# ScalarE seeds the next unit's accumulator before it squares and stores the last unit, in the first MLP layer of a gated FNet kernel

## The chip, the cores and the metric

The kernel runs on one core of a Trainium2 chip. The metric is the device time of one execution in microseconds (us), as the median of several runs. The engines are written as the profile has them: PE is TensorE's matmuls, PEld its weight loads, DVE is VectorE, ACT is ScalarE, and SP is the engine that issues most of the transfers.

## The reference

With S = 2048 tokens, D = 512 and F = 1792, all in float32, where `xn` is the layer-normalised input:

```python
xn = layernorm(x)
a, b = xn @ hid_re.T, xn @ hid_im.T
s = seq_re @ a - seq_im @ b
h = relu(xn @ w1 + b1) ** 2
out = x + s * silu(h @ w2 + b2)
```

The change lies in the line that computes `h`.

## The kernel before, in words

Every product of matrices is cut into blocks of 2 by 2 and computed with seven block products instead of eight, with sums of blocks on both sides. Each operand is held as a high and a low part, and each block product takes three passes (high by high, high by low, low by high). The stages follow one another on TensorE: layer norm and the first transform, the second transform, eight units of the hidden transform (`YUnit`), 28 units of the first MLP layer (`HUnit`), the second MLP layer with the gate, and a tail. The order of the instructions on each engine is the order in which the program is written, since the scheduler is set to manual. What an engine does beside the units is set by hand in tables (`H_SIDE` for this stage): names of steps that load an operand, form its sums and split it into high and low part. Of each operand ScalarE makes the high part (line 136) and VectorE then the low part (line 139).

**A unit of the first layer** covers two of the 14 blocks of 128 hidden features for one of the four chunks of 512 tokens: 4 chunks by 7 pairs make 28 units. Unit n has four accumulators of 256 columns in PSUM, A, B, C and D, and units of even and odd n use different banks. Its seven products, each of six matmuls of 256 columns on line 790, go to A (1, then 2), to D (7), to B (6, then 5, then 3) and to C (4). The sums between products are made by seeding: ScalarE copies minus A into B before product 6 is added on top (line 146, the step `seed("B", "A")`), and minus B into C before product 4. Below, these two are called seed B and seed C.

What is read out of a unit, all into a buffer `h` of four blocks:

- `m7`: ScalarE copies D (line 146).
- `c11`: ScalarE applies bias and relu to A after product 2 (line 848).
- `c22`: VectorE adds B after product 5 to what m7 left (line 860 or 800). Product 3 goes into the same accumulator, so it waits for c22.
- `c21`: VectorE subtracts C after product 4 (line 860 or 803).
- `c12`: ScalarE applies bias and relu to B after product 3 (line 848).
- For the eleven units in `ACT_PAIR` (4, 5, 6, 8, 10, 12, 14, 16, 18, 21, 25) ScalarE also does the relu of the two lower blocks (a second line 848, 512 columns) and squares all 1024 columns. For the others VectorE squares the lower two blocks (line 875), and ScalarE squares 512 columns.
- `square()`: that square on ScalarE (line 879), and behind it on ScalarE's queue the transfer of `h` to HBM (line 880), from where the second layer loads it (line 760).

**The loop over the units** interleaves two units. Pass n, here called round n, issues for unit n the products 1, 7, 6 and 2, and for unit n-1, named `before` in the code, the rest. TensorE's order in a round is product 1 of unit n, then 5 and 4 of n-1, then 7 and 6 of n, then 3 of n-1, then 2 of n. ScalarE's order in a round is seed B of n, c11 of n-1, the splits of the table's second column, m7 and seed C of n, c12 of n-1 (with the relu of the lower blocks), and last the square and the store of n-1. VectorE's order is c22 and c21 of n-1 and then the table's second column: low parts, and the sums for later ones. In the texts below T(n) is the time at which TensorE starts product 5 of unit n-1 in round n, right after product 1 of unit n.

Of the kernel before, what the change touches and what calls it, by code (L numbers as in the profile page):

```python
# [130 lines left out]
def fnet_gated_kernel(ctx, tc, x, xt, ct, wd, w1, w2, b1, b2, out):  # L131
# [274 lines left out]
    def go(*names):  # L406


        for v in names:
            if v[0] == "h" and int(v[1:]) >= NTC * NP:  # L410
                continue
            if v not in making:
                making[v] = makers[v[0]](int(v[1:]))
            next(making[v])
# [469 lines left out]
    def bias(m, n, cols=slice(0, 2)):  # L884

        m = m.rearrange("p (k e) -> p k e", k=2)[:, cols]
        b = BIASED[n] * 256
        copy(m, b2s[:, None, b:b + 256].to_broadcast([P, cols.stop - cols.start, 256]))

    def outer(m, k, n, cols=(0, 1)):  # L890

        p = n % NP
        a, b = PRODUCTS[k]
        for i in cols:
            for a_, b_ in PASSES:
                nc.tensor.matmul(m[:, i * 256:(i + 1) * 256], ready[n][:, a_, H_SLOT[a], i * P:(i + 1) * P],  # L896
                                 W2[p][:, b_, b], start=p == 0 and i == 0 and (a_, b_) == (HI, HI) and k not in BIASED,
                                 stop=p == NP - 1 and (a_, b_) == (LO, HI), skip_group_check=True)
# [59 lines left out]
    for u in range(2):  # L958
        unit = YUnit(u)
# [32 lines left out]
    before = None  # L992
    for u in range(2, NC):
        n = 2 * u + 2
        unit = YUnit(u)
# [26 lines left out]
        before = unit  # L1022


    class Banks(dict):
# [4 lines left out]
        def __missing__(self, k):  # L1030
# [2 lines left out]
            self[k] = bank(tag, f"m{k}_o{self.c}")  # L1033
            return self[k]

    for n in range(NTC * NP):
        unit = HUnit(n)
        first, second, later = H_SIDE.get(n, ((), (), ()))
        go(*first)
        unit.products(1)  # L1040
        unit.seed("B", "A")
        before.c11()
        before.products(5)
        before.c22()
        before.products(4)
        before.c21()
        go(*second)
        unit.products(7)
        unit.m7()
        unit.products(6)  # L1050
        unit.seed("C", "B")
        before.products(3)
        before.c12()
        if n == NTC * NP - 1:
            ms = Banks(0)
            for k in (2, 4):
                bias(ms[k], k)
        unit.products(2)
        before.square()
        go(*later)  # L1060
        before = unit

    outer(ms[1], 1, 0)
    before.c11()
    before.products(5)
    before.c22()
# [123 lines left out]
def _launch(arrays, out_shape):  # L1190
    import numpy as np
    import concourse.bacc as bacc
    from concourse.bass_utils import run_bass_kernel_spmd

    nc = bacc.Bacc("TRN2", target_bir_lowering=False, num_devices=1, dynamic_dma_scratch_size=1024)
    feed, args = {}, []
    for name, v in arrays.items():
        v = np.ascontiguousarray(v)
        feed[f"in_{name}"] = v
        args.append(nc.dram_tensor(f"in_{name}", v.shape, mybir.dt.from_np(v.dtype), kind="ExternalInput").ap())  # L1200
    args.append(nc.dram_tensor("out_0", out_shape, F32, kind="ExternalOutput").ap())
    with tile.TileContext(nc, schedule_with_timeline_sim=True) as tc:
        fnet_gated_kernel(tc, *args)
    r = run_bass_kernel_spmd(nc, [feed], core_ids=[0])
    return r.results[0]["out_0"]
# [25 lines left out]
```

## Time and profile before

| what | value |
|---|---|
| median of 3 runs | 673.04 us (672.74 to 673.34) |
| the profiled execution's own time | 672.81 us |
| its span, first to last instruction | 671.0 us |
| PE busy | 665.1 us, 99% of the span |
| DVE busy | 596.4 us, 89% |
| ACT busy | 380.2 us, 57% |
| first-layer rounds | 403 to 536 us of the span |

The profile is of one execution. A row of its timeline gives the start in us from the span's start, the duration, the engine, the line, the operation and the tiles it writes and reads; several equal instructions in a row are merged, with their count. In square brackets stands the idle time of the engine before the row and what ended it. The end of a matmul is modelled, so a group of matmuls reads a little longer than the distance to the next group's start.

### The profile page before, as it was taken

What the parts mean: (1) busy time and instruction counts of PE and PEld (TensorE: products, weight loads), DVE (VectorE), ACT (ScalarE), POOL (GpSimd) and SP (SyncE); (2) the same over time, 40 slices, a digit from 0 to 9 for tenths busy, and PEclk for the clock granted to TensorE, in tenths of its full rate; (3) what the DMA queues carried; (4) which work ended last, traced back from release to release, by engine and by line L of the source; (5) the groups of instructions that cost most, each with busy time, mean ns of one, the idle gap of its engine ahead of it and who ended that gap; (6) DMA issues with size and microseconds to landing.
All of it is one profiled execution on the core that took longest, in us unless ns stands there. A gap on an engine that the chain in (4) does not pass through costs nothing.

```text
span 671.0 us, 13184 instructions
## 1 busy us (share of the span) xinstructions
PE 665.1 (99%) x5437; PEld 646.3 (96%) x5437; DVE 596.4 (89%) x831; ACT 380.2 (57%) x524; POOL 8.8 (1%) x11
## 2 busy tenths in 40 slices
PE   9999999999999999999999999999999999999997
PEld 6888889999999999999999999999999999999997
DVE  7997888999999999899899988977877889999997
ACT  6855664634445454444464557888778865454451
POOL 0000000000000000000000000000000000101010
PEclk9999999999999999999999999999999999999999
DMA  8635497646556774759588558565755866777775
GB/s 292 226 115 206 145 347 269 220 142 224 200 167 226 252 282 162 262 186 346 184 303 278 181 189 317 202 251 205 271 182 198 324 243 214 190 218 190 219 205 156
DMA packets 51739, 150.82 MB, mean 225 GB/s; under 512 B 4960, under 2 KB 19552, under 8 KB 50272
## 3 DMA queue, kind: packets, MB, share of 16 engines
q1 hardware_dynamic: 43568, 129.28, 56.9%
q10 hardware_dynamic: 6208, 18.88, 7.1%
q0 software_dynamic: 1904, 1.84, 1.9%
q8 instruction: 42, 0.69, 0.4%
q14 instruction: 17, 0.14, 0.1%
HBM read 101.98 MB, written 47.99 MB: 223 GB/s over the span
## 4 chain that ended last, share of the span: by engine, by line
PE 96%; DVE 1%; ACT 1%; DMA 0%; issue 0%; ACTq 0%; SPq 0%; DVEq 0%
PE m L382 34%; PE m_o L896 15%; PE r_B L790 13%; PE r_A L790 9%; PE pq_b L397 8%; PE r_C L790 4%; PE r_D L790 4%; PE m_last L896 4%; PE pq_ba L397 2%; PE pq_bc L397 2%; PE pq_bb L397 2%; DVE z L1146 0%; DMA x<-in_x 0%; DVE z L946 0%; ACT h L848 0%
## 5 line engine op out<-in xcount | busy, mean ns | idle before, releaser
L382 PEld LDWEIGHTS m<-g,xc 128*128 128x128 f32 x2016 | 228.6, 188 | 0.1
L382 PE MATMUL m<-g,xc 128*128 128x256 f32 x2016 | 228.7, 276 | 0.0
L136 ACT ACTIVATE g<-u 128x1792 fp32r<-128x1792 f32 (+2 forms) x65 | 99.0, 1523 | 126.9 <-PE m L382 89.0
L139 DVE TENSOR_TENSOR g<-u,g 128x1792 fp32r<-128x1792 f32 (+2 forms) x66 | 116.9, 1772 | 19.8 <-ACT g L136 19.2
L896 PE MATMUL m_o<-w,g 128*128 128x256 f32 x882 | 100.5, 276 | 0.0
L896 PEld LDWEIGHTS m_o<-w,g 128*128 128x128 f32 x882 | 100.3, 188 | 0.0
L136 ACT ACTIVATE g<-hr 128x1792 fp32r<-128x1792 f32 (+2 forms) x31 | 48.2, 1565 | 40.0 <-PE m_o L896 16.8
L790 PE MATMUL r_B<-xT,w 128*128 128x256 f32 x504 | 66.6, 277 | 0.4 <-ACT r_B L146 0.4
L397 PE MATMUL pq_b<-g,xc 128*128 128x512 f32 x240 | 65.2, 391 | 0.4 <-DVE small L247 0.4
L790 PEld LDWEIGHTS r_B<-xT,w 128*128 128x128 f32 x504 | 61.5, 188 | 0.5 <-ACT r_B L146 0.5
L139 DVE TENSOR_TENSOR g<-hr,g 128x1792 fp32r<-128x1792 f32 (+2 forms) x31 | 56.7, 1837 | 2.9 <-ACT g L136 2.8
L397 PEld LDWEIGHTS pq_b<-g,xc 128*128 128x128 f32 x240 | 44.7, 188 | 10.7 <-ACT g L136 0.8
L790 PE MATMUL r_A<-xT,w 128*128 128x256 f32 x336 | 42.8, 276 | 0.0
L790 PEld LDWEIGHTS r_A<-xT,w 128*128 128x128 f32 x336 | 40.2, 188 | 0.0
L790 PE MATMUL r_B<-wdp,yg 128*128 128x256 f32 x288 | 35.8, 277 | 0.0
L304 DVE TENSOR_TENSOR u<-u 128x512 f32<-128x512 f32 x48 | 32.8, 684 | 1.9 <-DMA u<-in_ct 1.9
L790 PEld LDWEIGHTS r_B<-wdp,yg 128*128 128x128 f32 x288 | 34.1, 188 | 0.0
L896 PE MATMUL m_last<-w,g 128*128 128x256 f32 x294 | 33.5, 276 | 0.0
L896 PEld LDWEIGHTS m_last<-w,g 128*128 128x128 f32 x294 | 33.4, 188 | 0.0
L139 DVE TENSOR_TENSOR yg<-yraw,yg 128x1792 fp32r<-128x1792 f32 x13 | 26.2, 2018 | 0.6 <-ACT yg L136 0.6
L136 ACT ACTIVATE yg<-yraw 128x1792 fp32r<-128x1792 f32 x13 | 22.2, 1708 | 5.8 <-DVE yraw L313 5.3
L790 PE MATMUL r_D<-xT,w 128*128 128x256 f32 x168 | 23.6, 276 | 0.0
(192 smaller groups left out, 877.8 us busy)
## 6 DMA issues: line engine op xcount, KB each, us to landing
u<-in_ct SPq DMA_DIRECT2D x63, 512.0 KB, 3.8
hd<-h ACTq DMA_DIRECT2D x28, 512.0 KB, 3.9
hr<-hd SPq DMA_DIRECT2D x28, 512.0 KB, 3.8
wdp<-wdd SPq DMA_DIRECT2D x8, 896.0 KB, 6.5
yraw<-pqd SPq DMA_DIRECT2D x13, 512.0 KB, 5.9
pqd<-c SPq DMA_DIRECT2D x6, 1024.0 KB, 6.3
w<-w1d SPq DMA_DIRECT2D x6, 896.0 KB, 8.2
y<-y ACTq DMA_DIRECT2D x8, 512.0 KB, 5.2
```

Source lines behind the costliest of these rows:

```text
L136: nc.scalar.activation(hi, src, AF.Copy)
L139: nc.vector.tensor_tensor(lo, src, hi.bitcast(F32), op=ALU.subtract)
L304: nc.vector.tensor_tensor(t[:, 0:2], r[:, 0:1].to_broadcast([P, 2, 256]), r[:, 1:3], op=ALU.add)
L382: nc.tensor.matmul(ps[:, d], w[:, a_, d * P:(d + 1) * P], halves(mv(b_)), start=first and d == 0 and (a_, b_) == (HI, HI), stop=last and ( ...
L397: nc.tensor.matmul(accs[c][k], w, part[c, j][:, b_, 2 * h:2 * h + 2], start=j == 0 and h == 0 and (a_, b_) == (HI, HI), stop=j == NJ - 1 a ...
L790: nc.tensor.matmul(self.region(REGION[k]), w, mv, start=i == 0 and k in (1, 7), stop=i == len(ops) - 1, skip_group_check=True)
L896: nc.tensor.matmul(m[:, i * 256:(i + 1) * 256], ready[n][:, a_, H_SLOT[a], i * P:(i + 1) * P], W2[p][:, b_, b], start=p == 0 and i == 0 an ...
```

## The change

At the top of a round, the square and the store of a unit come behind the seed B of the unit two further on: the loop remembers one more unit, `behind`. In round n ScalarE now issues seed B of n, then the square and the store of unit n-2, then c11 of unit n-1 and the rest as before. The call at the end of the round goes away. For unit 26 the call stands behind the loop, and ScalarE's order there is the same as before. No instruction is added or removed.

```diff
+    behind = None
     for n in range(NTC * NP):
         unit = HUnit(n)
...
         unit.products(1)
         unit.seed("B", "A")
+        if behind:
+            behind.square()
         before.c11()
         before.products(5)
         before.c22()
...
         unit.products(2)
-        before.square()
         go(*later)
-        before = unit
+        before, behind = unit, before

     outer(ms[1], 1, 0)
+    behind.square()
     before.c11()
```

The first place is ScalarE in rounds 5 and 6. In the names, `r5_B` is accumulator B of unit 5, `h4` is the buffer that units 4 and 5 share, `xT2` and `xT3` are the input operands of the second chunk of tokens, and `hd` is the place of h in HBM. Before:

```order
L146 ACTIVATE r5_B_4737<-r5_A_4730 128x256
L848 ACTIVATE h4_4703<-r4_A_4666,b1s_65 128x256
L136 ACTIVATE xT2_4754<-xr2_4266 128x768
L136 ACTIVATE xT2_4754<-xs2_4691 128x1024
L146 ACTIVATE h4_4703<-r5_D_4765 128x256
L146 ACTIVATE r5_C_4779<-r5_B_4737 128x256
L848 ACTIVATE h4_4703<-r4_B_4673,b1s_65 128x256
L848 ACTIVATE h4_4703<-h4_4703,b1s_65 128x2x256
L879 ACTIVATE h4_4703<-h4_4703 128x1024
L880 DMA hd0_4_96<-h4_4703 128x1024
L146 ACTIVATE r6_B_4808<-r6_A_4801 128x256
```

And with the change:

```order
L146 ACTIVATE r5_B_4735<-r5_A_4728 128x256
L879 ACTIVATE h2_4579<-h2_4579 128x2x256
L880 DMA hd0_3_95<-h2_4579 128x1024
L848 ACTIVATE h4_4703<-r4_A_4664,b1s_65 128x256
L136 ACTIVATE xT2_4754<-xr2_4266 128x768
L136 ACTIVATE xT2_4754<-xs2_4691 128x1024
L146 ACTIVATE h4_4703<-r5_D_4765 128x256
L146 ACTIVATE r5_C_4779<-r5_B_4735 128x256
L848 ACTIVATE h4_4703<-r4_B_4671,b1s_65 128x256
L848 ACTIVATE h4_4703<-h4_4703,b1s_65 128x2x256
L146 ACTIVATE r6_B_4806<-r6_A_4799 128x256
```

The seed of `r6_B` now follows unit 4's relu directly, and the square and store of unit 3 have come in between the seed of `r5_B` and everything else of round 5: c11 of unit 4, the two splits of `xT2`, and seed C.

The second place is ScalarE in rounds 22 and 23, where `g0` and `g1` are the first operands of the second layer, split in two parts. Before:

```order
L146 ACTIVATE r23_B_5878<-r23_A_5871 128x256
L848 ACTIVATE h22_5845<-r22_A_5806,b1s_65 128x256
L136 ACTIVATE g1_5896<-hr1_1_5618 128x1024
L136 ACTIVATE g1_5896<-hr1_0_5617 128x768
L146 ACTIVATE h22_5845<-r23_D_5901 128x256
L146 ACTIVATE r23_C_5915<-r23_B_5878 128x256
```

And with the change:

```order
L146 ACTIVATE r23_B_5876<-r23_A_5869 128x256
L879 ACTIVATE h20_5717<-h20_5717 128x1024
L880 DMA hd3_0_113<-h20_5717 128x1024
L848 ACTIVATE h22_5845<-r22_A_5804,b1s_65 128x256
L136 ACTIVATE g1_5896<-hr1_1_5616 128x1024
L136 ACTIVATE g1_5896<-hr1_0_5615 128x768
L146 ACTIVATE h22_5845<-r23_D_5901 128x256
L146 ACTIVATE r23_C_5915<-r23_B_5876 128x256
```

Here a square of 1024 columns (unit 21 is in `ACT_PAIR`) and its store stand between seed B and seed C of the same unit.

## Rows read from the trace of the kernel before

**Rows 1.** The page, part 1: busy time, share of the span, instructions.

```profile
PE 665.1 (99%) x5437; PEld 646.3 (96%) x5437; DVE 596.4 (89%) x831; ACT 380.2 (57%) x524; POOL 8.8 (1%) x11
```

**Rows 2.** Waits of PE in the span: total us, times, longest us.

```profile
PE r_B L790 <- ACT r_B L146: 0.4, 1, 0.4
```

**Rows 3.** Timeline of PE and PEld, rounds 6 and 7.

```profile
426.70 0.84 PE L790 MATMUL r_B<-xT,w 128*128 128x256 f32 x6
...
428.74 1.52 PE L790 MATMUL r_B<-xT,w 128*128 128x256 f32 x12
...
431.46 0.84 PE L790 MATMUL r_B<-xT,w 128*128 128x256 f32 x6
...
434.02 1.66 PE L790 MATMUL r_B<-xT,w 128*128 128x256 f32 x12 [0.35 <-ACT r_B L146]
435.52 1.52 PE L790 MATMUL r_A<-xT,w 128*128 128x256 f32 x12
...
428.63 1.43 PEld L790 LDWEIGHTS r_B<-xT,w 128*128 128x128 f32 x12
...
434.02 1.46 PEld L790 LDWEIGHTS r_B<-xT,w 128*128 128x128 f32 x12 [0.55 <-ACT r_B L146]
```

**Rows 4.** Timeline of ACT, from the end of round 4 to round 7.

```profile
421.29 0.63 ACT L879 ACTIVATE h<-h 128x512 f32<-128x512 f32 x1
...
422.33 0.37 ACT L146 ACTIVATE r_B<-r_A 128x256 f32<-128x256 f32 x1 [0.40 <-PE r_A L790]
422.61 0.47 ACT L848 ACTIVATE h<-r_A,b1s 128x256 f32<-128x256 f32 x1
422.96 0.85 ACT L136 ACTIVATE xT<-xr 128x768 fp32r<-128x768 f32 x1
...
424.91 0.39 ACT L146 ACTIVATE r_C<-r_B 128x256 f32<-128x256 f32 x1
425.54 0.47 ACT L848 ACTIVATE h<-r_B,b1s 128x256 f32<-128x256 f32 x1 [0.24 <-PE r_B L790]
425.92 0.72 ACT L848 ACTIVATE h<-h,b1s 128x512 f32<-128x512 f32 x1
426.66 1.06 ACT L879 ACTIVATE h<-h 128x1024 f32<-128x1024 f32 x1
427.76 0.33 ACTq L880 DMA_DIRECT2D hd<-h  x1
428.13 0.37 ACT L146 ACTIVATE r_B<-r_A 128x256 f32<-128x256 f32 x1 [0.40 <-ACT h L879]
...
433.60 0.37 ACT L146 ACTIVATE r_B<-r_A 128x256 f32<-128x256 f32 x1 [0.40 <-ACT h L879]
```

**Rows 5.** Timeline of DVE in rounds 5 and 6, five instructions left out.

```profile
423.85 0.96 DVE L139 TENSOR_TENSOR xT<-xr,xT 128x768 fp32r<-128x768 f32 x1
...
428.71 0.42 DVE L800 TENSOR_TENSOR h<-r_B,h 128x256 f32<-128x256 f32 x1
```

**Rows 6.** Timeline of ACT and DVE in rounds 2 and 3.

```profile
409.17 1.71 ACT L136 ACTIVATE w<-w1raw 128x1792 fp32r<-128x1792 f32 x1 [0.36 <-DVE w1raw L313]
...
410.91 2.02 DVE L139 TENSOR_TENSOR w<-w1raw,w 128x1792 fp32r<-128x1792 f32 x1
...
414.37 0.48 DVE L860 SCALAR_TENSOR_TENSOR h<-r_B,b1s,h 128x256 f32<-128x256 f32 x1
```

**Rows 7.** Timeline of ACT and DVE in rounds 8 and 9.

```profile
438.94 1.70 ACT L136 ACTIVATE w<-w2raw 128x1792 fp32r<-128x1792 f32 x1
...
440.67 2.03 DVE L139 TENSOR_TENSOR w<-w2raw,w 128x1792 fp32r<-128x1792 f32 x1 [1.02 <-ACT w L136]
...
443.75 0.42 DVE L800 TENSOR_TENSOR h<-r_B,h 128x256 f32<-128x256 f32 x1
```

**Rows 8.** Timeline of SP and DVE: a stored h loaded again, and used.

```profile
513.98 0.37 SPq L760 DMA_DIRECT2D hr<-hd  x1
...
532.35 0.68 DVE L310 TENSOR_TENSOR hr<-hr 128x512 f32<-128x512 f32 x1
```

## The prediction

> **What bounds the kernel now.** I read the page's busy times first. TensorE is busy 99% of the span [rows 1], so only a stall of TensorE, or the end of one, can move the time. The list of waits comes second: in the 28 rounds of this stage TensorE waits once, on a ScalarE write to accumulator B [rows 2]. The timeline of TensorE, third, shows the place and the price. A round is 42 matmuls in 4.76 us (T(6) = 426.70, T(7) = 431.46 [rows 3]), 0.68 us per product and 1.36 per group of twelve. Product 6 starts 2.04 after T (426.70, 428.74), so in round 7 it was due at 431.46 + 2.04 = 433.50. It started at 434.02, and the group after it at 435.52 instead of 434.86. **The stall cost 0.66 us.** The timeline of ScalarE, fourth, says why: seed B of unit 7 ran from 433.60 to 433.97, behind the relu, square and store of a unit in `ACT_PAIR` [rows 4].
>
> From this stall I take the rule for all others. The weight load stood still too, and for 0.55 us [rows 3]; it normally leads its matmul by 0.11 (428.63, 428.74). It began 0.05 after the seed's end. So a late operand costs: its end, plus 0.05, minus the due time of the weight load, plus 0.03 for the restart. Here that is 434.02 - 433.39 + 0.03 = 0.66.
>
> **What the change removes.** Seed B no longer stands behind a square (1.10 us up to the store's issue, [rows 4]: 426.66, 427.76) and the issue (0.37: 427.76, 428.13). It then follows product 1 at once. The end of product 1 reads T + 0.16 (a group of twelve reads 1.52 and the next starts after 1.36), and ScalarE starts 0.04 after a TensorE end (c12 at 425.54, its product from 428.74 - 4.76 = 423.98, reading 1.52). So seed B starts at T + 0.20 where ScalarE is free, far ahead of T + 2.04. **The stall of 0.66 goes.** That is all there is to gain; where seeds were late by less (428.13 in round 6) TensorE did not wait.
>
> **What it adds.** ScalarE used the time before product 1 ended to square and issue. Now it waits there, and square and issue come after seed B, ahead of c11, the splits and seed C. Its steps, start to start, from [rows 4]: seed 0.28 (422.33, 422.61); square of 512 columns 0.66 (0.63 and the 0.04 before an issue); square of 1024 columns 1.10; issue 0.37; c11 0.35 (422.61, 422.96); a split in two parts with m7 behind it 1.95 (422.96, 424.91). Two kinds of deadline come after that, and I went through all rounds for both.
>
> *Kind one: c22, through VectorE.* VectorE's low part waits for ScalarE's high part, c22 of the next round stands behind it in VectorE's queue, and product 3 waits for c22. Product 3's weight load is due 0.68 - 0.11 after the start of its group, in round 6 at 428.74 + 0.57 = 429.31.
>
> - Unit 5. In round 5, T = 421.94. Seed 422.14, square 422.42, issue 423.08, c11 423.45, split of `xT2` 423.80 instead of 422.96. Its end is 424.65, VectorE starts at 424.69 instead of 423.85 [rows 5]. From there to c22 of unit 5 VectorE runs seven instructions without a gap, so c22 moves from 428.71 to 429.55 and ends at 429.97. Stall: 430.02 - 429.31 + 0.03 = **0.74**.
> - Unit 2. In round 2, T = 407.66 (two rounds before 417.18, itself two before T(6)). c11 at 409.17, split at 409.52 instead of 409.17; its low part at 409.52 + 1.71 + 0.04 = 411.27 instead of 410.91, and c22 of unit 2 at 414.73 instead of 414.37 [rows 6]. It ends at 415.21; due 429.31 - 3 x 4.76 = 415.03. Stall: **0.26**.
> - Units 8 and 14, alike. T(8) = 435.52 + 1.36 = 436.88. A square of 1024: split at T + 0.20 + 0.28 + 1.10 + 0.37 + 0.35 = 439.18 instead of 438.94; VectorE waited for this split already (1.02 us idle), so c22 moves by 0.24 to 443.99 and ends at 444.41 [rows 7]. Due: 436.88 + 4.76 + 2.04 + 0.57 = 444.25. Stall 0.24 each, **0.48**.
>
> *Kind two: seed C.* It reads B, and product 5 of the next round adds to B, so product 5's weight load, due at T + 4.65, waits for it. With a square of 1024 and a split in two parts, seed C starts at T + 0.20 + 0.28 + 1.10 + 0.37 + 0.35 + 1.95 = T + 4.25 and releases at T + 4.25 + 0.39 + 0.05 = T + 4.69.
>
> - Rounds 10, 12, 16 and 18: late by 0.04, which costs 0.07 with the restart. That is within what 0.01 us rows can tell, so I take 0.03 each, **0.12**, between 0 and 0.28.
> - Rounds 23 and 27. The round before also has a split in two parts (with a square of 512, seed C at T + 3.81), then c12 (0.28 later, as a seed), the second relu (0.38 later: 425.54, 425.92) and 0.62 for it (0.72 less an overlap of 0.10), so seed B starts at T + 0.33 and everything 0.13 later: 0.17 + 0.03 = 0.20 each, **0.40**.
>
> The stores go out 0.5 to 1.1 us later in 26 rounds, on ScalarE's queue. The loads of h that follow have cover: unit 2's is issued at 513.98 and used at 532.35 [rows 8]. Were that gone, a load would delay VectorE's sums and then TensorE, 1 us at most. SP's queue keeps its order, so I cost this at nothing. Seed B also waits for the c12 before it on its own engine now, which ends before product 1 in all rounds but the ones above; nothing.
>
> **The sum.** 0.74 + 0.26 + 0.48 + 0.12 + 0.40 = 2.00 us of new stalls, less 0.66, is **+1.3 us**. After this stage TensorE runs without a wait to the tail, so the shift stays. Against the profiled execution's 672.81 that makes 674.15; the median of the runs is 0.23 above that execution, so **674.4 us**.
>
> One price is open: how soon the square may start behind the seed. No row has that pair. If it starts as c11 does behind a seed, it is 0.28, which I take, since both read what nobody is writing. If it had to wait for the seed's end and a hand-over (0.37 + 0.04), each of the ten late places would be 0.13 later, +1.3 us more. If ScalarE did not stand still for the issue (0.37), only unit 5 would be late, by 0.37.
>
> **A measurement of this kernel can tell about 0.2%, 1.35 us, from no change.** My sum lies on that bound.
>
> **The rivals.**
> 1. *The weight load goes ahead of the wait.* The matmul alone would wait, and each stall would be 0.14 smaller: 0.60 + 0.12 + 0.20 + 0.12 + 0 = 1.04, net +0.4, 673.4 us. Against it: in the one stall on record the weight load stood still for 0.55 us [rows 3]. That row is of a wait on ScalarE; none is of a wait on VectorE in these rounds. [...] Chance 0.12.
> 2. *Not slower: the issue does not hold ScalarE.* If the next activation passes the waiting store, c11 and the splits come 0.37 earlier; only unit 5 stalls, by 0.37, and the net is -0.3, 672.7 us. It decides at 0.37 us in unit 5's chain. Against it: in [rows 4] the activation behind an issue always starts after it (427.76, 428.13), with the square before it as the releaser. With no new stall at all it is 672.4, still no 0.2%. Chance 0.08.
> 3. *The square waits for the seed.* Ten places 0.13 later each: 675.7 us. For it: nothing shown; against it, c11 overlaps a seed in every round. Chance 0.13.
> 4. *Something outside the stage gains*, over 1.35 us: I see no cause. Chance 0.02. That the change does nothing is excluded by the order of the instructions.
>
> **How the numbers follow.** The forecast has 0.65. Ten places read to about 0.05 each, partly together, give it 673.8 to 675.0, about half above 674.39, the bound. Slower: 0.34 of the forecast and rival 3, 0.47. Within 0.2%: 0.31, 0.12 and 0.08, 0.51. Faster: 0.02. The range leaves out rival 2, most of rival 4 and the upper part of rival 3: 673.3 to 675.4.
>
> **What would show it.** In the profile of the changed kernel the wait at product 6 of unit 7 is gone, and seed B starts about 0.2 us after T in most rounds. TensorE's waits are on VectorE at product 3 of units 5 (the longest, about 0.7), 2, 8 and 14, and on ScalarE's seed C at product 5 after rounds 23 and 27. VectorE's idle time behind ScalarE's splits grows. I am wrong in kind if TensorE has no wait on VectorE there, or if a wait shows up in the second layer; wrong in size only if the places are these and the sum is not about 2 us.

## The result and the profile after

The changed kernel takes **675.98 us** (median of 6 runs, 675.46 to 676.71), the kernel before 673.22 in the same comparison: a ratio of 1.0042 (95% interval 1.0029 to 1.0055). It is slower, by 2.8 us where +1.3 was forecast, and lies 0.6 us above the top of the range (675.4).

The page's first part, of the changed kernel, for PE:

```profile
PE 668.3 (99%) x5437; PEld 647.7 (96%) x5437; DVE 596.4 (88%) x831; ACT 379.3 (56%) x524; POOL 8.8 (1%) x11
```

Against [rows 1] the other engines did the same work in nearly the same time (ScalarE 0.9 us less); TensorE's 5437 matmuls read 3.2 us more. The span is 674.3 us (671.0 before). The waits of PE and PEld between 400 and 545 us, in the changed kernel (total us, times, longest):

```profile
PE r_B L790 <- DVE h L800: 0.5, 1, 0.5
...
PEld r_B L790 <- DVE h L800: 0.9, 2, 0.7
PEld r_B L790 <- ACT r_C L146: 0.4, 2, 0.2
PEld r_B L790 <- DVE h L860: 0.2, 1, 0.2
```

The wait on seed B [rows 2] is gone. In its place stand waits on VectorE's c22 (lines 800 and 860) and on seed C, as forecast. How much of the time lies in the stage is read from two groups of TensorE's timeline, the first product 5 (round 1) and product 3 of unit 27, the last product of the stage. Of the kernel before:

```profile
402.90 0.84 PE L790 MATMUL r_B<-xT,w 128*128 128x256 f32 x6
...
534.91 0.87 PE L790 MATMUL r_B<-xT,w 128*128 128x256 f32 x6
```

and of the changed kernel, with rounds 6 and 12 between:

```profile
403.52 0.84 PE L790 MATMUL r_B<-xT,w 128*128 128x256 f32 x6
...
429.69 0.84 PE L790 MATMUL r_B<-xT,w 128*128 128x256 f32 x6
431.04 0.96 PE L790 MATMUL r_B<-xT,w 128*128 128x256 f32 x6 [0.52 <-DVE h L800]
...
462.33 0.97 PE L790 MATMUL r_B<-xT,w 128*128 128x256 f32 x6
463.14 0.87 PE L790 MATMUL r_C<-xT,w 128*128 128x256 f32 x6
463.85 0.87 PE L790 MATMUL r_D<-xT,w 128*128 128x256 f32 x6
...
538.20 0.87 PE L790 MATMUL r_B<-xT,w 128*128 128x256 f32 x6
```

The distance of the two groups, **the stage's length** from here on, is 132.01 us before and 134.68 after: +2.67, nearly all of the 2.8. (The spans of the two traces differ by 3.3. The other 0.6 lies ahead of the stage, where both kernels run the same instructions: the first product 5 starts at 402.90 and 403.52, and between 402.80 and 403.52 in all traces of this case. So kernels are compared by the stage's length.) Two things are to be seen in the middle rows. Product 3 of unit 5 (431.04), due at 429.69 + 0.68 = 430.37, is late by 0.67, and its second matmul by another 0.11, 0.78 in all: the largest new stall, forecast at 0.74. And in round 12 the groups behind a small wait (462.33) stay 0.71 us apart (463.14, 463.85), where a group of six otherwise takes 0.68. The single matmuls' starts in the trace say it more finely: 113.4 ns from one to the next (the mean of the stage that has no wait, below), but 117.7 ns behind this wait, for 40 matmuls. That was in no row the prediction used. Below, such a run of matmuls is called a slow stretch.

Summed over the stage from these single starts: the waits come to 2.34 us after and 0.63 before (+1.71), and the time of the slow matmuls above 113.4 ns each to 1.09 us after and 0.15 before (+0.94). Together +2.65.

A slow stretch doesn't need a wait. Of the 0.15 us before, 0.11 lies at the end of the stage, where the first matmuls of the second layer (line 896) come in between. In the kernel before, no wait stands ahead of these groups, and they are 0.70 to 0.71 apart:

```profile
531.40 0.87 PE L896 MATMUL m_o<-w,g 128*128 128x256 f32 x6
532.11 0.87 PE L790 MATMUL r_B<-xT,w 128*128 128x256 f32 x6
532.81 0.87 PE L790 MATMUL r_C<-xT,w 128*128 128x256 f32 x6
```

In all thirteen traces of this case a stretch begins at this same matmul: the group of six on the line of the second layer reads 0.87 us in each, where one at the usual pace reads 0.84.

### The profile page after: what moved, and what is told of

Its sections match the earlier page's. It is cut to its first block, busy times and chain, and to the rows that moved or that the text cites. A ratio compares the mean times of both kernels' runs of the same rounds, so it can differ in the third digit from the quotient of the medians.

```text
span 674.3 us, 13210 instructions
## 1 busy us (share of the span) xinstructions
PE 668.3 (99%) x5437; PEld 647.7 (96%) x5437; DVE 596.4 (88%) x831; ACT 379.3 (56%) x524; POOL 8.8 (1%) x11
## 4 chain that ended last, share of the span: by engine, by line
PE 96%; DVE 1%; DMA 1%; ACT 1%; issue 0%; SPq 0%; DVEq 0%
PE m L382 34%; PE m_o L896 15%; PE r_B L790 14%; PE r_A L790 9%; PE pq_b L397 8%; PE r_C L790 4%; PE r_D L790 4%; PE m_last L896 4%; PE pq_ba L397 2%; PE pq_bc L397 1%; PE pq_bb L397 1%; DMA x<-in_x 1%; DVE z L1149 0%; DVE z L946 0%; DVE z L951 0%
## 5 line engine op out<-in xcount | busy, mean ns | idle before, releaser
L790 PE MATMUL r_B<-xT,w 128*128 128x256 f32 x504 | 68.4, 279 | 0.6 <-DVE h L800 0.5
L790 PE MATMUL r_C<-xT,w 128*128 128x256 f32 x168 | 23.8, 277 | 0.0
```

Source lines behind the costliest of these rows:

```text
L790: nc.tensor.matmul(self.region(REGION[k]), w, mv, start=i == 0 and k in (1, 7), stop=i == len(ops) - 1, skip_group_check=True)
```

## The experiments

### 1. The change cut into three parts

Each unit's square moves behind the next seed only if its number is in a set; the others stand as before.

```diff
-        if behind:
+        if behind and behind.n in LATE:
             behind.square()
...
         unit.products(2)
+        if before.n not in LATE:
+            before.square()
```

`LATE` was (5) for the first kernel, (0, 3, 5, 6, 12) for the second, (5, 8, 10, 14, 16, 21, 25) for the third, and all but (0, 3, 6, 8, 10, 12, 14, 16, 21, 25) for the fourth.

> The new order for one square alone: unit 5's, which moves behind seed B of unit 7; all other squares stand as before. Every theory expects the stall of 0.66 us at product 6 of unit 7 to go and no other to come, so 0.7 us less than before, about 672.5 us, and no wait of TensorE in the 28 rounds. If the time stays, the stall was not worth its length.

> The new order for unit 5's square and for those of units 0, 3, 6 and 12, which make product 3 of units 2, 5, 8 and 14 late through VectorE. By the prediction's rule (end + 0.05 - due + 0.03) these cost 0.26 + 0.74 + 0.48 = 1.48 us, less 0.66: 0.8 us above before, 674.0 us. If a late operand also costs a second gap of 0.11 us and a stretch of slower matmuls, as TensorE's start times in the changed kernel's trace suggest (0.33, 0.80, 0.36 and 0.35), it is 1.84 less 0.66: 1.2 us above before, 674.4 us.

> The new order for unit 5's square and for those of units 8, 10, 14, 16, 21 and 25, which make only seed C late, by little. By the prediction's rule they cost 0.12 + 0.40 = 0.52 us, less 0.66: 0.1 us below before, 673.1 us. If a short wait is followed by a long stretch of slower matmuls, each place costs 0.15 to 0.35 us, as in the changed kernel's trace (about 1.3 in sum), and it is 0.6 us above before, 673.8 us; the trace then shows the distance between groups of six longer than 0.68 us well after each wait.

> The complement: the new order for all squares but those of units 0, 3, 6, 8, 10, 12, 14, 16, 21 and 25. If the late places are all that costs, it is as with unit 5's square alone, 0.7 us below before, 672.5 us, with no wait in the rounds. If the later stores or their traffic cost something of their own, it is 0.5 us or more above that, with TensorE's groups slower in rounds without a wait.

| LATE | median us | ratio to before (95%) | stage's length, us |
|---|---|---|---|
| before | 673.25 | | 132.01 |
| unit 5 | 672.41 | 0.9993 (0.9985 to 1.0002) | 131.35 |
| and late through VectorE | 674.25 | 1.0018 (1.0009 to 1.0027) | 133.25 |
| and late seed C | 674.06 | 1.0012 (1.0003 to 1.0021) | 132.60 |
| the rest | 674.15 | 1.0015 (1.0006 to 1.0024) | 132.66 |

*Unit 5 alone.* No wait is left in the stage, and its two groups are 0.66 us nearer than before, the length of the one stall removed:

```profile
403.22 0.84 PE L791 MATMUL r_B<-xT,w 128*128 128x256 f32 x6
...
534.57 0.87 PE L791 MATMUL r_B<-xT,w 128*128 128x256 f32 x6
```

This is all that the move has to give, in a version whose stage is shorter than both kernels'. Its interval holds 1, so the time alone doesn't show the gain; the trace does.

*Late seed C.* All six places wait, four forecast at 0.03 us and two (rounds 23 and 27) at 0.20. These two wait 0.10 and 0.07 here: the squares of units 20 and 24 stand as before, so the rounds ahead of them don't push their seed B, as the forecast has it for the whole change. But over the run with unit 5 alone the stage is 1.25 us longer, not 0.52. The timeline of TensorE in round 12 of this kernel:

```profile
460.40 0.96 PE L791 MATMUL r_B<-xT,w 128*128 128x256 f32 x6
461.20 0.87 PE L791 MATMUL r_C<-xT,w 128*128 128x256 f32 x6
461.91 0.87 PE L791 MATMUL r_D<-xT,w 128*128 128x256 f32 x6
```

The group at 460.40 is followed after 0.80 instead of 0.68: 0.10 is the wait (its second matmul comes 213 ns after the first), and from there on the groups are 0.71 apart. The first five waits are 0.10 each, and 22, 40, 29, 29 and 28 matmuls at 117.7 ns follow them (the sixth wait is that after round 27). So in the four small places both terms are too small in the prediction: the wait (0.10, not 0.04) and what follows it (0.10 to 0.17 us, not 0.03).

The clock is not the cause. The same trace in two windows, one at the normal and one at the slower pace (length, busy time of PE, PEld, DVE, ACT and POOL with their instructions, granted clock, DMA share, GB/s):

```profile
455.00:459.70 4.70, 4.70 (x44) 4.70 (x43) 3.04 (x6) 3.97 (x7) 0.00 (x0) 1.00 0.71 206
460.70:465.30 4.60, 4.60 (x41) 4.60 (x40) 3.79 (x7) 3.23 (x8) 0.00 (x0) 1.00 0.66 228
```

The granted clock is 1.00 in both. The DMA engines are less busy in the slower window (0.66 against 0.71) and move a little more (228 against 206 GB/s).

*Late through VectorE.* Over the run with unit 5 alone the stage is 1.90 us longer, where 1.48 was forecast. But this kernel is not a clean sum. With unit 3's square moved and unit 4's not, both fall into round 5, so that seed B of unit 6 is late by 0.50 (product 6 waits), and unit 5's product 3 by less for it (0.27).

*The rest* missed what it was built for, by the same trap. All theories said 672.5; it took 674.15. Where a square that moves is followed by one that doesn't, one round has two squares on ScalarE. The timeline of ACT in round 22, and of PE in round 23:

```profile
504.18 0.62 ACT L880 ACTIVATE h<-h 128x512 f32<-128x512 f32 x1
...
508.95 1.06 ACT L880 ACTIVATE h<-h 128x1024 f32<-128x1024 f32 x1
...
510.41 0.37 ACT L147 ACTIVATE r_B<-r_A 128x256 f32<-128x256 f32 x1 [0.40 <-ACT h L880]
...
510.83 0.86 PE L791 MATMUL r_B<-xT,w 128*128 128x256 f32 x5 [0.23 <-ACT r_B L147]
```

Seed B of unit 23 ends at 510.78 (510.41 + 0.37), late behind a square and a store's issue, as [rows 4] showed it for unit 7. There are two such waits of 0.50 and one of 0.10 on a seed C, with 0.2 us more of slow matmuls: 1.3 of the 1.31 us that this stage is longer than with unit 5 alone. Nothing is left for the later stores or their traffic.

### 2. Does the length of a wait set what follows it?

The waits above suggested that short ones bring the long stretches. To set waits by hand, a base without the squares and without the second relus in `ACT_PAIR` (left out of the computation) gives ScalarE room, and repeated seeds C make product 5 late in seven rounds.

```diff
         unit.products(6)
+        for cols in AGAIN.get(n, ()):
+            copy(unit.region("C")[:, 0:cols], unit.region("B")[:, 0:cols], -1.0)
         unit.seed("C", "B")
```

> The kernel before without the squares and without the second relus of the units in ACT_PAIR (left out of the computation; the stores stay), so that ScalarE has room in all rounds. All theories expect no wait of TensorE in the 28 rounds, as in the run with unit 5's square alone, and a time within 0.3 us of it (672.4 us); it is the base for the two ladders.

> The base without squares, with seed C repeated in rounds 7, 9, 11, 13, 15, 17 and 19, so that seed C releases product 5 late by a ladder of lengths: by the prediction's durations -0.05, 0.00, 0.05, 0.11, 0.22, 0.39 and 0.67 us in this order (to about 0.05). By the prediction's rule the stalls are these plus 0.03 where they are late, 1.6 us in all, with no change of pace behind them. If a short wait is followed by a long slow stretch and a long wait is not, the rounds behind 11 and 13 show 13 matmuls or more at 117 to 118 ns, those behind 17 and 19 fewer than 7. If the place decides, and not the length, the stretch behind a round is the same as in the ladder turned round.

> The same ladder turned round: 0.67, 0.39, 0.22, 0.11, 0.05, 0.00 and -0.05 us late in rounds 7, 9, 11, 13, 15, 17 and 19. By the prediction's rule 1.6 us again and no change of pace. If the length decides, the long slow stretches now lie behind rounds 13 and 15 and those behind 7 and 9 are short; if the place decides, the same rounds as in the first ladder have them.

The base took 672.28 us, with a stage of 131.35 us, to 0.01 that with unit 5's square alone. The ladders took 678.72 and 678.86 us (these kernels and those of the next two ladders ran once each): a repeated seed overwrites what the one before it wrote, waits for its end on ScalarE's own semaphore, and starts 0.40 us behind it, not 0.28. So all rungs were long waits, 0.53 to 1.50 us, and 8 of the 14 were followed by at most 3 slow matmuls. That fits the theory of the length. But behind round 15 there were 37 in both ladders, after waits of 0.94 and 0.64 us.

### 3. A finer ladder, and the seed's second wait

> The base without squares with seed C repeated over fewer columns, so that seed C ends late at product 5 after rounds 7, 9, 11, 13, 15, 17 and 19 by -0.03, 0.02, 0.07, 0.13, 0.18, 0.24 and 0.02 us (from the first ladder's 0.40, 0.35, 0.29 and 0.24 us for 256, 192, 128 and 64 columns and a normal lead of 1.31). If a wait costs its length and no more, TensorE's group is late by just these. If short waits are the ones followed by long slow stretches, most of the six late places show 13 slow matmuls or more, where the first ladders had 6 of 14. If the length of a stretch hangs on the place, a stretch behind round 15 has 37 again.

> The same turned round: 0.02, 0.24, 0.18, 0.13, 0.07, 0.02 and -0.03 us. If the place decides how long a stretch is, two stretches behind the same round are of the same length in both kernels; if the wait's length decides, they go with the lengths and are turned round too.

They took 673.85 and 673.55 us. Wait in us / slow matmuls behind it, by single starts:

| after round | 7 | 9 | 11 | 13 | 15 | 17 | 19 |
|---|---|---|---|---|---|---|---|
| ladder | 0.53 / 0 | 0.59 / 0 | 0.64 / 0 | 0.69 / 3 | 0.94 / 37 | 1.09 / 0 | 1.50 / 41 |
| turned | 1.50 / 82 | 1.02 / 13 | 0.94 / 11 | 0.69 / 0 | 0.64 / 37 | 0.59 / 0 | 0.53 / 0 |
| fine | none / 0 | 0.02 / 14 | 0.08 / 11 | 0.13 / 23 | 0.19 / 35 | 0.23 / 23 | 0.02 / 42 |
| fine, turned | 0.02 / 80 | 0.17 / 13 | 0.19 / 10 | 0.13 / 23 | 0.08 / 35 | 0.02 / 24 | none / 0 |

Read by columns: in these four kernels, **where a stretch comes, its length belongs to the place**, to within 2 matmuls, for waits from 0.02 to 1.50 us. It ends at the same matmul of the program, to within 3. Read by rows: of the 12 waits up to 0.23 us each was followed by one; of the 14 longer ones six were (a seventh by 3 slow matmuls). A wait of 0.02 us was followed by 80 matmuls at the slower pace, 0.35 us. Behind round 15, in the first ladder and in the fine one turned round (waits of 0.94 and 0.08), the same pace:

```profile
477.77 0.98 PE L791 MATMUL r_B<-xT,w 128*128 128x256 f32 x6 [0.66 <-ACT r_C L147]
478.58 0.87 PE L791 MATMUL r_C<-xT,w 128*128 128x256 f32 x6
479.29 0.87 PE L791 MATMUL r_D<-xT,w 128*128 128x256 f32 x6
```

```profile
475.33 0.94 PE L791 MATMUL r_B<-xT,w 128*128 128x256 f32 x6
476.11 0.87 PE L791 MATMUL r_C<-xT,w 128*128 128x256 f32 x6
476.82 0.87 PE L791 MATMUL r_D<-xT,w 128*128 128x256 f32 x6
```

and behind round 13, in the first ladder, a wait without a stretch (groups 0.68 apart):

```profile
467.30 0.96 PE L791 MATMUL r_B<-xT,w 128*128 128x256 f32 x6 [0.42 <-ACT r_C L147]
468.11 0.84 PE L791 MATMUL r_C<-xT,w 128*128 128x256 f32 x6
468.79 0.84 PE L791 MATMUL r_D<-xT,w 128*128 128x256 f32 x6
```

The other question was why seed C was late by 0.10. In the changed kernel's timeline of ACT in round 2, T(2) being 403.52 + 4.76 = 408.28, seed B starts at T + 0.26, where the prediction had T + 0.20:

```profile
408.54 0.37 ACT L146 ACTIVATE r_B<-r_A 128x256 f32<-128x256 f32 x1 [0.94 <-PE r_A L790]
408.82 0.62 ACT L879 ACTIVATE h<-h 128x512 f32<-128x512 f32 x1
409.47 0.34 ACTq L880 DMA_DIRECT2D hd<-h  x1
409.86 0.48 ACT L848 ACTIVATE h<-r_A,b1s 128x256 f32<-128x256 f32 x1 [0.42 <-ACT h L879]
```

The compiled order says what differs. Before, the square stands ahead of the seed and carries the wait for c12 on ScalarE's own semaphore; after, the seed carries two waits (the square and the seed of round 2, before, then after):

```
L879 ACTIVATE h_4443<-h_4443 128x2x256 [waits Activation_49]
L146 ACTIVATE r_B<-r_A 128x256 [waits PE_49]

L146 ACTIVATE r_B<-r_A 128x256 [waits PE_49,Activation_49]
L879 ACTIVATE h_4443<-h_4443 128x2x256
```

In the changed kernel's trace these two waits are not on one instruction: in each of the 26 rounds the wait for TensorE (semaphore 103) stands in a semaphore instruction of its own, ahead of the seed, which keeps the wait on ScalarE's own (101). The trace's instructions of line 146 between 400 and 545 us (count, then shortest, median and longest in ns) show 26 more of them, one for each moved square, in the kernel before and then the changed one:

```profile
L146 ACTq EVENT_SEMAPHORE  x11: 17/38/38, 419.1 to 523.7; - x11
```

```profile
L146 ACTq EVENT_SEMAPHORE  x37: 17/17/38, 408.5 to 530.6; - x37
```

So the change adds no instruction in the program's text, but 26 in ScalarE's queue. In the round above the semaphore instruction starts at 408.48, 0.311 us after the start of product 1's last matmul, and the seed at 408.54, 0.061 behind it. In 16 of the 26 rounds the seed starts 0.061 or 0.062 us behind it; in the other ten (0.069 to 0.327) the relu ahead of it had not ended when the semaphore instruction started. In rounds 0 and 1, where the seed waits for TensorE alone, it starts 0.312 to 0.314 us after that matmul in the kernel before and in the changed one.

To test it, a copy of one column of c12's output onto itself takes that wait over, ahead of the seed, while ScalarE stands idle.

```diff
+        if isinstance(behind, HUnit):
+            copy(behind.out(C12)[:, 0:1], behind.out(C12)[:, 0:1])
         unit.seed("B", "A")
```

> The changed kernel with one instruction more in each round: a copy of one column in place on ScalarE, ahead of seed B, that takes over the wait for c12 of two rounds ago, so that seed B waits for TensorE alone. If the second wait costs (seed B starts 0.26 us after T where the prediction had 0.20), seed B starts 0.06 earlier, the waits at the ten late places shrink by 0.06 each, 0.5 to 0.6 us in all, and the time falls to about 675.4 us, lower where a stretch of slow matmuls goes too. If seed B is later for another reason, nothing falls, and the copy changes nothing: 676.0 us.

> The run with seed C alone late (squares of units 5, 8, 10, 14, 16, 21 and 25 moved), with the same one-column copy ahead of seed B. If the second wait is what made seed C late by 0.10 where the prediction had 0.04, the waits shrink from 0.10 to 0.04 us each. If a slow stretch follows any wait, however short, and ends at a place of its own, the stretches stay as long as they were (22, 40, 29, 29 and 28 matmuls), and the time falls by 0.3 us only, to 673.8 us; if it needs a wait of some length, they go and the time is about 673.0 us.

The changed kernel with the copy takes 675.26 us (1.0029, 1.0018 to 1.0040), 0.7 less than without it. The two intervals overlap, so it is the stage that shows the gain: 134.14 instead of 134.68. Its timeline of ACT, with T(2) = 402.80 + 4.76 = 407.56:

```profile
406.90 0.20 ACT L146 ACTIVATE h<-h 128x1 f32<-128x1 f32 x1
407.75 0.37 ACT L146 ACTIVATE r_B<-r_A 128x256 f32<-128x256 f32 x1 [0.65 <-PE r_A L790]
408.04 0.62 ACT L879 ACTIVATE h<-h 128x512 f32<-128x512 f32 x1
```

The seed starts at T + 0.19. Measured from the start of product 1's last matmul it is 0.313 us in this kernel and 0.373 without the copy, and line 146 has 11 semaphore instructions again. **The second wait cost 0.06 us**, and one copy more in each of 26 rounds made the stage shorter. The waits at units 2, 5 and 8 and after rounds 12 and 18 shrink by 0.06 to 0.07 each; after rounds 23 and 27 they grow by 0.02, and at unit 14 by 0.06, where the slow stretch ahead of product 3 is gone. Of the 0.54 us, 0.25 is waiting (0.5 to 0.6 was expected), and about as much is fewer slow matmuls. With seed C alone late, the copy takes the waits from 0.10 to 0.05 (forecast: 0.04), the stage from 132.60 to 132.04, and the time to 673.68 us (1.0004, 0.9995 to 1.0013). The stretches were 0, 41, 29, 11 and 13, against 22, 40, 29, 29 and 28: they did not all stay, as one theory had it, nor go with the shorter wait, as the other had. TensorE's instructions are the same in both kernels, so what the ladders showed does not hold here: neither the place alone nor the length of the wait decides a stretch. Round 12 of the two kernels with the copy, the changed one first, shows that a wait of 0.05 can go either way at one place:

```profile
461.27 0.90 PE L790 MATMUL r_B<-xT,w 128*128 128x256 f32 x6
462.01 0.84 PE L790 MATMUL r_C<-xT,w 128*128 128x256 f32 x6
462.69 0.84 PE L790 MATMUL r_D<-xT,w 128*128 128x256 f32 x6
```

```profile
460.58 0.91 PE L791 MATMUL r_B<-xT,w 128*128 128x256 f32 x6
461.32 0.87 PE L791 MATMUL r_C<-xT,w 128*128 128x256 f32 x6
462.02 0.87 PE L791 MATMUL r_D<-xT,w 128*128 128x256 f32 x6
```

## Why the prediction was wrong, point by point

**Right: what bounds it, what goes, where the larger new stalls come.** The stall of 0.66 us went, and by itself that is -0.66 (unit 5 alone). The nine places that wait by more than 0.02 us are forecast ones, on the forecast engines. The square starts 0.28 behind the seed (408.54, 408.82), so rival 3 is out, though its time, 675.7, is the nearest. The issue holds ScalarE (409.47 to 409.86, 0.39, forecast 0.37), so rival 2 is out. The weight load stands still before a late product 3 or 5 (PEld waited 0.7 us for c22 of unit 5 and up to 0.2 for a seed C), so rival 1 is out.

**Right in size, once the seed has one wait.** In the changed kernel with the copy the stalls through VectorE are 0.72, 0.24, 0.21 and 0.22 us (units 5, 2, 8 and 14). The prediction's 0.74, 0.26, 0.24 and 0.24 hold 0.03 each for the restart; without it they are 0.71, 0.23, 0.21 and 0.21. Of its four small seeds C the three that are late are late by 0.04 to 0.05 (forecast 0.04). (Round 16 has no wait: TensorE is itself later by then, since the slow stretch behind unit 14's wait runs through that round.) Rounds 23 and 27 read 0.29 and 0.27, forecast 0.17: there ScalarE has no idle time ahead of the seed, and the copy pushes it (in round 23 the relu at 509.36 for 0.73 us, the copy at 509.98, the seed at 510.07).

**Wrong, step one.** "Seed B also waits for the c12 before it on its own engine now, which ends before product 1 in all rounds but the ones above; nothing." The work it waits for is done long before, but the second wait puts a semaphore instruction ahead of the seed and delays it by 0.06 us (0.373 instead of 0.313 us after the start of product 1's last matmul). Square, store, c11, split and seed C stand behind it and come that much later. The waits sum to 2.34 us. The forecast's 2.00 hold 0.03 for the restart at six places, so its waits are 1.82: +0.52. By place, units 2, 5 and 8 and rounds 12 and 18 wait 0.06 to 0.08 more, and there the copy takes 0.06 to 0.07 off again: at these five the second wait is shown to be the cause. Rounds 23 and 27 wait 0.10 and 0.07 more. That the second wait does it there too is argued and not shown, since the copy, which has no idle time to run in, makes these two longer. Round 10 waits only 0.02 more, unit 14 0.05 less and round 16 0.03 less: there TensorE is itself in a slow stretch or right behind one. Three places that the forecast doesn't name (product 5 of units 8, 14 and 20) add 0.01 to 0.02 each.

**Wrong, step two.** The rule's last term, "plus 0.03 for the restart", was read from one stall, and in it the stretch behind the wait is short (5 matmuls, 0.02 us in [rows 3]). In the changed kernel the nine places have stretches of 2 to 53 matmuls behind them, one more of 23 follows a wait of 0.015 us (product 5 of unit 14), and slow matmuls cost 0.94 us more than before, where the restarts of the forecast come to 0.18 less the 0.03 of the stall removed: +0.79. With the first step that is 1.34 + 0.52 + 0.79 = 2.65, against 2.67 measured for the stage.

What the runs leave open is what the slower pace is. They exclude the clock (1.00 at both paces in the run with seed C late), the length of a wait as what sets the length of a stretch, and later stores as a cost of their own. A wait is not needed for a stretch either: one begins at the same matmul near the end of the stage in every trace, without a wait. What starts a stretch there, what ends one, and what decides that a wait has none, wasn't found.

## What to carry to other kernels

On an engine that is busy 99% of the time, the price of a late operand can be its lateness and a tail: here a wait of 0.02 us had 80 slow matmuls behind it and came to 0.37 us in all. So a move that removes one stall and makes nine others, some late by only a few hundredths of a microsecond, can lose; move only what cures the stall (here the square of one unit) and leave the rest.

Look at what semaphores an instruction waits on after a move. A wait that an earlier instruction used to absorb may fall onto one that is on the path, and cost even though it has long been met: here the seed's wait for TensorE then stood in an instruction of its own in ScalarE's queue (17 ns), and the seed started 0.06 us later. A small instruction ahead of it, in idle time, can take it back: here a copy of one column (0.20 us) did.

## What the runs showed that was not expected

- TensorE ran this stage at two paces at the same granted clock (1.00): 113.4 and 117.7 ns from one matmul of 256 float32 columns to the next, with the weight load 110 and 115 ns ahead of its matmul (before and changed kernel). Behind waits it went on at the slower one for 2 to 82 matmuls: after all 12 set waits of 0.02 to 0.23 us, and after six of the 14 of 0.53 to 1.50. It also did so without a wait, at one place of the stage, in every trace.
- A second semaphore wait, met long before, delayed seed B by 0.06 us (0.373 against 0.313 us after the start of product 1's last matmul): in the changed kernel the wait for TensorE stands in a semaphore instruction of its own (17 ns), and the seed starts 0.061 or 0.062 us after that one's start in 16 of 26 rounds.
- In the first ladder a repeated seed of 256 columns, which overwrites the output of the one before it and waits for that on ScalarE's own semaphore, starts 0.40 us behind it; in the changed kernel the square behind a seed, without such a wait, 0.28 (408.54, 408.82).
